# First four tiles loaded with four tokens to a partition, v regrouped by selection matmuls, masks multiplied, new order

## The chip, the cores and the metric

One core of a Trainium2 chip runs the whole program. The metric is the device time of one execution in microseconds. The kernel before takes 180.32 us, the median of three runs (180.25 to 180.33).

## The reference

The program computes attention with a local window and a few global keys, and puts its output through a feed-forward layer that takes the largest of three products.

```python
scores = scale * np.matmul(q, k.transpose(0, 1, 3, 2))
...
is_global = pos[None, :] < int(n_global)
is_local = (rel >= 0) & (rel < int(n_local))
keep = is_global | is_local
dist = np.where(is_global & ~is_local, float(n_local), np.abs(rel).astype(np.float32))
slopes = 2.0 ** (-8.0 * (np.arange(H, dtype=np.float32) + 1) / H)
bias = -slopes[:, None, None] * dist[None, :, :]
...
h = np.maximum(np.maximum(x @ w1, x @ w2), x @ w3)
return (h @ w_out).astype(np.float32)
```

q, k and v are 4 batches x 8 heads x 768 tokens x 64, in float32. n_global is 8 and n_local is 96, so a query sees the 96 keys up to itself and the first eight. The scores get the bias, keys that are not kept get none of the weight, and a softmax follows. The attention output of all heads of a token is a row x of 512. w1, w2, w3 are 512 x 768 and w_out is 768 x 512.

## The kernel before, in words

**Tiles.** The 3072 tokens are 24 tiles of 128, six to a batch. Because the window is shorter than a tile, a tile's queries need two blocks of keys only: the tile itself, and the tile before it, whose first eight keys are overwritten by the batch's first eight (the global ones; `put_kg`, `put_vg`, L209 to L221). Tiles are grouped into chunks for the feed-forward layer: `sizes` 4, 2, 2, 4, 4, 4, 4.

**Order.** There is no scheduler. A string, `SCHEDULE` (L25 on), lists the units one after the other, and a loop at the end (L475) calls the function of each with its numbers. Every engine takes its instructions in that order. The last number of a unit mostly picks the engine that copies: 0 is ACT, 1 is DVE, 2 is POOL (GpSimd). A unit for loads puts its DMA into SP's queue; TensorE's instructions of a later unit wait behind those of an earlier one.

**Units.** The ones that the change and the prediction touch:

- `l` (`load_part`, L151) loads q or k of a group of tiles with `sz` tokens to a partition. Before, the groups begin with two of two tiles, so that a partition's piece in the memory is 512 bytes. `c` (`cast_part`, L178) casts it to bf16; `x` (`u_x`, L226) transposes it on TensorE (L239) and copies it from PSUM with the tokens put back in order (L243) into `qkT`, which holds q and k of a batch with the head's 64 elements across partitions, two heads above each other (`jp` is such a pair of heads).
- `L`, `C`, `X` do the same for single tiles from tile 12 on, with 256-byte pieces; X with a last number of 4 transposes by DMA.
- `v` (`load_v`, L169) loads v of a tile, one token to a partition (256-byte pieces), `C` with a 1 casts it into `va`, which has 65 columns to a head: 64 of v and a one, whose product is the sum of the weights.
- `K` (`u_K`, L297) makes the multiplicative mask of a head, exp of minus slope times distance, with a large distance where a key is not kept. `B` (`u_B`, L291) makes the same as an additive bias.
- `S` (`u_S`, L268) computes a tile's scores for four heads (L283) and takes the exponential (L288). With a last number of 1 it first puts the bias into PSUM by two matmuls with the identity (L275); otherwise `M` (`u_M`, L302) multiplies the mask afterwards. Of the eight half tiles of tiles 0 to 3, six get the bias.
- `A` (`u_A`, L311) multiplies the weights with v (L322, L325), divides by the sums (L331, L332) and leaves `xb`. `T` (`u_XT`, L335) transposes xb into `xT`, on TensorE or by DMA.
- `F` c.f.j (`u_F1`, L355) is a group of four matmuls (L361) of chunk c, for 128 of the 768 columns (f) of weight j. The three results are cast (ACT, L366) and maximised (DVE, L368, L370). `O` (`u_F2`) is the last product (L376) of a tile and its output; `E` the outputs of the last chunk.
- `w` and `W` load and cast the weights: `w`0.j brings the first 256 columns of weight j, `w`1.j the other 512; `o` and `Q` those of w_out.
- `D` issues matmuls on zeros.

**Buffers.** Scores and the products of `A` take turns in two PSUM tiles, `sp0` and `sp1`. All else on TensorE uses three buffers `h` and one `tp`. A matmul into such a buffer waits until its last content was copied out.

Of the kernel before, what the change touches and what calls it, by code (L numbers as in the profile page):

```python
# [12 lines left out]
FP32 = mybir.dt.float32  # L13
# [12 lines left out]
    K0 K1 K2 K3 K4 K5 l1.0 l1.1 D0.3 c0.0.2 B0.1 B1.1 B2.1 B3.0 K6 B4.1 B5.1 c0.1.1 c1.0.2 x0.0.4 B6.1  # L26
    B7.1 x0.1.4 S0.0.1 v0 l2.0 l2.1 K7 S0.1.1 G0.0 S1.0.1 S1.1.0 x1.0.3 c1.1.2 M0.0 M0.1 M1.0 v1 x1.1.4
    C0.1.2 v2 A0.1 G1.2 S2.0.1 M1.1 c2.0.2 x2.0.1 C1.1.1 S2.1.0 G2.2 S3.0.1 M2.0 M2.1 C2.1.1 T0.1 S3.1.1
    M3.0 M3.1 c2.1.2 v3 A1.0 C3.1.0 w0.0 V1.2 x2.1.2 w1.0 A2.1 V2.2 A3.0 T1.0 T2.1 T3.1 W1.0.1 W0.0.0
    G3.2 S4.0.0 S4.1.0 F0.0.0 F0.1.0 M4.0 F0.2.0 F0.3.0 G4.1 S5.0.0 M4.1 S5.1.0 w0.1 W0.1.1 w0.2 W0.2.2  # L30
    V3.2 F0.0.1 F0.1.1 F0.0.2 F0.1.2 v4 C4.1.0 A4.0 V4.2 w1.1 W1.1.2 W2.0.0 F0.4.0 F0.5.0 M5.0 M5.1 w1.2
    W1.2.2 v5 W2.1.0 T4.0 F0.2.1 F0.3.1 l3.0 l3.2 F0.4.1 l3.1 c3.0.2 c3.2.2 F0.5.1 o2 C5.1.0 A5.1 l3.3
    F0.2.2 Q2.2 F0.3.2 W2.2.0 o0 T5.0 F0.4.2 o1 F0.5.2 x3.0.0 F1.0.0 F1.1.0 c3.1.1 F1.2.0 x3.2.0 Q0.2
    F1.0.1 F1.1.1 F1.2.1 l4.0 l4.1 c3.3.0 F1.0.2 F1.1.2 F1.2.2 x3.1.2 x3.3.1 F1.3.0 F1.4.0 Q1.2 F1.3.1
    S6.0.0 S6.1.0 v6 v7 v8 G6.0 F1.3.2 F1.5.0 v9 c4.0.1 F1.4.1 S7.0.0 S7.1.0 G7.2 v10 M6.0 M6.1 M7.0
    M7.1 O0.0.0 F1.4.2 c4.1.1 C6.1.2 C7.1.2 L12 F1.5.1 S8.0.0 S8.1.0 x4.0.0 O0.1.0 A6.0 x4.1.2 A7.1 V7.2
    F1.5.2 v11 T6.0 O0.2.0 T7.1 G8.2 C8.1.2 S9.0.0 S9.1.0 G9.1 v12 v13 O0.3.0 F2.0.0 F2.1.0 S10.0.0 M8.0
    M8.1 M9.0 M9.1 S10.1.0 C9.1.2 L13 L14 F2.0.1 F2.1.1 F2.0.2 A8.0 C12.0.1 F2.1.2 G10.2 O1.0.0 V8.2
    A9.1 X12.1 M10.0 M10.1 C10.1.0 C11.1.0 F2.2.0 S11.0.0 S11.1.0 M11.0 M11.1 L15 F2.3.0 F2.4.0 O1.1.0
    V9.2 A10.1 F2.2.1 V10.2 T8.0 F2.3.1 F2.5.0 T9.0 A11.1 F2.4.1 T10.0 F2.2.2 F2.3.2 T11.1 F2.4.2  # L40
    S12.0.0 S12.1.0 F2.5.1 C13.0.2 C14.0.2 C15.0.1 X13.4 F3.0.0 F3.1.0 F3.0.1 G12.1 C12.1.0 F3.2.0
    F3.1.1 F3.2.1 S13.0.0 S13.1.0 F2.5.2 v14 C13.1.0 C14.1.2 M12.0 M12.1 F3.0.2 F3.1.2 X14.4 F3.2.2
    X15.4 G13.2 M13.0 M13.1 S14.0.0 S14.1.0 F3.3.0 F3.4.0 F3.5.0 M14.0 M14.1 G14.1 A12.0 A13.1 F3.3.1
    F3.4.1 F3.5.1 S15.0.0 M15.0 S15.1.0 G15.0 v15 V13.2 L16 L17 v16 T12.4 v17 M15.1 O2.0.0 C15.1.0 A14.0
    V14.2 F3.3.2 F3.4.2 T13.4 F3.5.2 C16.1.0 C16.0.2 X16.3 T14.4 C17.0.2 A15.1 X17.4 O2.1.0 S16.0.0
    S16.1.0 G16.1 L18 V15.2 L19 T15.1 M16.0 O3.0.0 M16.1 F4.0.0 F4.1.0 F4.0.1 F4.1.1 C18.0.2 L20 C19.0.2
    A16.1 F4.2.0 F4.3.0 S17.0.0 S17.1.0 F4.2.1 F4.0.2 F4.3.1 v18 M17.0 v19 M17.1 X18.3 X19.4 C20.0.0
    V16.2 F4.1.2 C17.1.2 O3.1.1 A17.1 F4.2.2 F4.3.2 S18.0.0 M18.0 S18.1.0 M18.1 F4.4.0 T16.4 T17.4
    F4.4.1 C18.1.2 C19.1.1 F4.4.2 X20.4 G18.1 S19.0.0 S19.1.0 F4.5.0 L21 M19.0 M19.1 v20 F4.5.1 A18.0
    T18.4 F4.5.2 A19.1 T19.4 V19.1 C21.0.1 X21.4 G19.1 L22 C22.0.2 L23 X22.4 O3.2.1 O3.3.0 O4.0.1  # L50
    S20.0.0 S20.1.0 M20.0 G20.0 O4.1.0 F5.0.0 F5.1.0 F5.2.0 S21.0.0 S21.1.0 G21.2 F5.0.1 F5.1.1 M20.1
    M21.0 F5.3.0 F5.0.2 F5.1.2 F5.2.1 F5.2.2 v21 C20.1.1 C21.1.2 F5.4.0 S22.0.0 M21.1 S22.1.0 C23.0.0
    F5.3.1 M22.0 M22.1 F5.5.0 F5.3.2 A20.0 V20.2 G22.2 v22 F5.4.1 X23.4 v23 F5.5.1 T20.4 A21.1 V21.1
    T21.4 F5.4.2 F5.5.2 S23.0.0 S23.1.0 M23.0 O4.2.0 M23.1 C22.1.2 A22.0 C23.1.0 O4.3.0 V22.2 T22.4
    A23.1 T23.4 O5.0.1 O5.1.0 O5.2.1 O5.3.0 F6.0.0 F6.1.0 F6.0.1 F6.0.2 F6.2.0 F6.3.0 F6.4.0 F6.1.1
    F6.2.1 F6.1.2 F6.3.1 F6.4.1 F6.2.2 F6.3.2 F6.5.0 F6.4.2 F6.5.1 F6.5.2 E
# [4 lines left out]
def kernel(  # L61
# [13 lines left out]
    nc = tc.nc  # L75
# [13 lines left out]
    sizes = [4, 2, 2, 4, 4, 4, 4]  # L89

    GROUPS = [[0, 2], [2, 2], [4, 2], [6, 4], [10, 2]]
# [8 lines left out]
    NSTART = sizes[0]  # L100
# [21 lines left out]
    zeros = persist.tile([128, 512], BF16, name="zeros")  # L122
# [3 lines left out]
    bias = persist.tile([128, 2, 2, 2, 3, 128], BF16, name="bias")  # L126
    NVA = 4
    va_ring = [persist.tile([128, H * 65], BF16, name=f"va{i}") for i in range(NVA)]
    va_first = [persist.tile([128, H * 65], BF16, name=f"vaf{i}") for i in range(2)]
    kg8 = [persist.tile([128, NP, NG], BF16, name=f"kg8_{i}") for i in range(2)]  # L130
# [5 lines left out]
    va, masked = {}, {}  # L136
# [7 lines left out]
    def part(n, s):  # L144

        T0, sz = GROUPS[n]
        jn = {2: 4, 4: 2, 6: 1}[sz]
        a, x = divmod(s, 4 // jn)
        return divmod(T0, NT) + (sz, a, x * jn, jn)
# [35 lines left out]
    def cast(T, what, how):  # L185
# [8 lines left out]
        if how == 3:  # L194
            nc.vector.tensor_copy(qk[:, 0], flat[:, 0])
            nc.gpsimd.tensor_copy(qk[:, 1], flat[:, 1])
        else:
            copies[how](qk, flat)  # L198
# [103 lines left out]
    def u_M(T, g):  # L302
        P = Pt[T, g]
        if masked[T, g]:
            return
# [204 lines left out]
```

The softmax here doesn't subtract the row's maximum and nothing guards it: scores larger than these inputs give would overflow.

## Time and profile before

| what | value |
|---|---|
| median of three runs | 180.32 us |
| profiled execution: span from the first to the last instruction | 178.5 us |
| time of the profiled execution itself | not listed apart; its span is 1.8 us short of the median |
| PE busy | 167.1 us, 94% |
| DVE busy | 119.1 us, 67% |
| ACT busy | 103.2 us, 58% |
| POOL busy | 37.4 us, 21% |
| read from HBM | 25.17 MB |
| mean granted TensorE clock | 0.997 |

The profile is of one execution. Its page gives each engine's busy time, the span in 40 slices of 4.46 us with a digit for the busy share in tenths, the DMA queues, the chain of waits (from the last instruction back to what released it, step by step), and groups of instructions with count, busy time, mean duration in ns and the idle time before them. PE are matmuls, PEld weight loads, which run beside them. Matmuls overlap, so that their spacing in the chain tells more than their duration: a 128x512 one lasts 379 ns by the group, while eight in a row take 1.73 us in the chain, 216 ns each.

### The profile page before, as it was taken

The numbers are of one execution on the slowest core, as the hardware profiler recorded it, in microseconds if no ns is written. First come the engines' busy times: TensorE is split into PE (matmuls) and PEld (weight loads), VectorE is DVE, ScalarE is ACT, GpSimd is POOL, SyncE is SP. The second block draws the span as 40 slices with busy tenths as digits, with TensorE's granted clock in tenths as the row PEclk, the third lists the DMA queues.
The fourth block names the chain that finished last, engine by engine and source line by source line (L and its number), as shares of the span: only waits on it lengthen the run. The fifth ranks groups of instructions, "written<-read, shape, count | busy, mean of one in ns | idle before, by whom it ended". The sixth has DMA issues, their size and how long they took to land.

```text
span 178.5 us, 3963 instructions
## 1 busy us (share of the span) xinstructions
PE 167.1 (94%) x1529; PEld 95.9 (54%) x1551; DVE 119.1 (67%) x237; ACT 103.2 (58%) x160; POOL 37.4 (21%) x65
## 2 busy tenths in 40 slices
PE   3599799999999999999999999999999999999991
PEld 0455645458866677845555555454454555444451
DVE  4519975977796689748978448978358986137610
ACT  4867898646689958555753936351862543440131
POOL 4255203543343012210006024100020401000000
PEclk9999999999999999999999999999999999999998
DMA  5999999999998899899544999988989664700015
GB/s 139 292 270 243 357 321 383 319 361 356 252 194 229 218 254 227 142 204 234 92 90 122 167 253 231 145 172 152 182 156 300 123 129 147 252 12 4 0 47 190
DMA packets 83587, 35.52 MB, mean 199 GB/s; under 512 B 66160, under 2 KB 78320, under 8 KB 83568
## 3 DMA queue, kind: packets, MB, share of 16 engines
q1 hardware_dynamic: 83424, 35.20, 83.6%
q8 instruction: 12, 0.20, 0.5%
q10 hardware_dynamic: 144, 0.07, 0.1%
q14 instruction: 7, 0.06, 0.1%
HBM read 25.17 MB, written 6.29 MB: 176 GB/s over the span
## 4 chain that ended last, share of the span: by engine, by line
PE 88%; ACT 3%; DVE 2%; POOL 2%; issue 1%; DMA 1%; POOLq 0%; ACTq 0%
PE h L361 53%; PE po L376 16%; PE sp L283 7%; PE op L322 3%; PE op L325 3%; PE tpp L239 3%; PE xtp L349 2%; ACT wmask L300 2%; PE sp L275 2%; DMA out_dram<-ost 1%; DVE qkT L243 1%; DVE xb L332 1%; ACT ost L382 1%; ACT P L288 1%; PE tp L261 1%
## 5 line engine op out<-in xcount | busy, mean ns | idle before, releaser
L361 PE MATMUL h<-xT,w 128*128 128x512 bf16 (+1 forms) x491 | 99.2, 348 | 0.7 <-issue 0.2
L361 PEld LDWEIGHTS <-w 128*128 128x128 bf16 x504 | 47.0, 98 | 40.4 <-ACT w L427 0.2
L288 ACT ACTIVATE P<-sp 128x1024 bf16<-128x1024 f32 (+1 forms) x48 | 43.4, 954 | 20.4 <-PE sp L283 20.2
L368 DVE TENSOR_TENSOR h<-h,h 128x512 bf16<-128x512 bf16 (+1 forms) x42 | 25.2, 609 | 25.6 <-PE h L361 15.5
L366 ACT CAST h<-h 128x512 bf16<-128x512 f32 (+1 forms) x42 | 21.6, 532 | 21.5 <-PE h L361 21.3
L376 PE MATMUL po<-wo,ht 128*128 128x512 bf16 (+2 forms) x147 | 33.1, 362 | 0.5
L370 DVE TENSOR_TENSOR ht<-h,h 128x512 bf16<-128x512 bf16 (+1 forms) x42 | 25.0, 606 | 3.7 <-PE h L361 3.0
L307 DVE TENSOR_TENSOR P<-P,wmask 128x1024 bf16<-128x1024 bf16 x36 | 24.8, 716 | 3.6 <-ACT P L288 3.5
L382 ACT COPY ost<-po 128x512 f32<-128x512 f32 (+2 forms) x20 | 11.2, 564 | 18.4 <-PE po L376 11.2
L376 PEld LDWEIGHTS <-ht 128*128 128x128 bf16 x156 | 14.0, 98 | 13.8
L332 DVE TENSOR_TENSOR xb<-op,rz 128x512 bf16<-128x512 f32 x24 | 16.6, 691 | 0.8
L283 PEld LDWEIGHTS <-qkT 64*128 64x128 bf16 x352 | 10.2, 96 | 10.0 <-issue 8.0
L283 PE MATMUL sp<-qkT 64*128 64x128 bf16 x352 | 15.2, 223 | 0.4 <-DVE xb L332 0.4
L322 PEld LDWEIGHTS <-P 128*128 128x128 bf16 x192 | 12.5, 97 | 2.7 <-ACT P L288 0.2
L221 POOL COPY va<-vaf 8x260 int32<-8x260 int32 x14 | 6.3, 449 | 34.7 <-PE op L325 34.7
L198 POOL CAST qkb<-raw 128x1024 bf16<-128x1024 f32 x7 | 7.2, 1037 | 27.6 <-DMA raw<-in_k_dram 27.6
L322 PE MATMUL op<-va,P 128*128 128x65 bf16 x160 | 12.4, 193 | 0.3 <-ACT va L189 0.2
L239 PE MATMUL tpp<-identb,qkp 128*128 128x128 bf16 x96 | 8.5, 246 | 4.0 <-POOL qkp L183 3.5
L325 PEld LDWEIGHTS <-P 128*128 128x128 bf16 x160 | 10.4, 97 | 1.8 <-issue 0.2
L239 PEld LDWEIGHTS <-qkp 128*128 128x128 bf16 x96 | 7.0, 112 | 5.8 <-POOL qkp L183 4.4
L325 PE MATMUL op<-va,P 128*128 128x65 bf16 x128 | 9.9, 193 | 0.1
L243 ACT COPY qkT<-tpp 128x1024 bf16<-128x1024 bf16 (+1 forms) x9 | 7.9, 873 | 3.4 <-PE tpp L239 3.4
(66 smaller groups left out, 107.7 us busy)
## 6 DMA issues: line engine op xcount, KB each, us to landing
rawv<-in_v_dram SPq DMA_DIRECT2D x24, 256.0 KB, 4.9
out_dram<-ost SPq DMA_DIRECT2D x23, 256.0 KB, 2.3
rawp<-in_q_dram SPq DMA_DIRECT2D x6, 512.0 KB, 7.3
rawp<-in_k_dram SPq DMA_DIRECT2D x6, 512.0 KB, 7.7
wst<-in_moe_w_dram SPq DMA_DIRECT2D x3, 1024.0 KB, 10.3
raw<-in_q_dram SPq DMA_DIRECT2D x12, 256.0 KB, 4.2
raw<-in_k_dram SPq DMA_DIRECT2D x12, 256.0 KB, 4.7
wst<-in_moe_w_dram SPq DMA_DIRECT2D x3, 512.0 KB, 8.6
```

What stands on the lines that cost most here:

```text
L239: nc.tensor.transpose(tp[:, e, j - lo], qb["p", n, s][:, e, 2 * j:2 * j + 2].rearrange("i h d -> i (h d)"), identb)
L283: nc.tensor.matmul(sp[:, hh, j2, ds], qT(T - ds, 1)[hsl, jp], qT(T, 0)[hsl, jp], start=not how, stop=True, skip_group_check=True)
L288: nc.scalar.activation(P[:, :, 0:n], sp.rearrange("p a b d n -> p (a b) d n")[:, :, 0:n], AF.Exp, bias=0.0, scale=scale)
L307: nc.vector.tensor_mul(P, P, wmask[:, g, :, 0:2])
L322: nc.tensor.matmul(o, P[:, i, 0], heads(va[T])[:, h], start=True, stop=(t == 0), skip_group_check=True)
L325: nc.tensor.matmul(o, P[:, i, 1], heads(va[T - 1])[:, h], start=False, stop=True, skip_group_check=True)
L332: nc.vector.tensor_tensor(out=x.rearrange("p (g h) d -> p g h d", g=2), in0=o4[:, :, :, 0:64], in1=rz[:, :, :, None].to_broadcast([128, 2, ...
L361: nc.tensor.matmul(ps, w123[f // 2][:, dm, j, (f % 2) * 128:(f % 2) * 128 + 128], xT[c][:, dm], start=(dm == 0), stop=(dm == 3))
L366: nc.scalar.copy(h01, ps)
L368: nc.vector.tensor_max(h01s[c, f], h01s[c, f], ps)
L370: nc.vector.tensor_max(ht[c][:, f], h01s[c, f], ps)
L376: nc.tensor.matmul(po, ht[c][:, f, tt * 128:(tt + 1) * 128], wo[:, f, cols], start=(f == 0), stop=(f == NF - 1))
```

## The change

The first group becomes four tiles (0 to 3) with four tokens to a partition: `GROUPS` begins with `[0, 4]`. q and k of it are loaded in eight pieces of a pair of heads, and a partition's piece is 1024 bytes. k is put in order of tokens when it is copied from PSUM, as before; q stays in the order of its four interleaved parts, and the scores' matmuls read 4 x 32 columns of it. v of these tiles is loaded likewise (`y`, `Y`), and a tile's 128 tokens are then picked out by matmuls with a matrix `sel` of zeros and ones, eight of 256 columns to a tile (`z`). New units compute scores and exponentials for two tiles and one pair of heads together (`s`), copy the global keys (`g`) and multiply the masks (`m`, on DVE or POOL). The additive bias is gone: all weights are multiplied with masks, `M` and `m`. `A` may use two `h` buffers instead of a score tile (last number 2).

The first two chunks of four and two tiles become four of two tiles, `sizes` 2, 2, 2, 2, 4, 4, 4, 4; neighbouring ones share their xT and ht tiles. The zeros of `D` shrink, and 36 matmuls of 128 columns stand at the head of TensorE's order, three more a little later. The first two loads move into the order, and all of the order is written anew. Of the later transposes, one tile's q and k, not three, and output transposes of eleven tiles, not thirteen, are left to TensorE; the rest goes by DMA. The function of the last outputs (`E`) stays.

The beginning of the new order, to the first groups of the feed-forward layer:

```
l0.4 l0.5 D5.36 K4 K1 K6 c0.4.1 l0.0 c0.0.2 K5 x0.4.2 c0.5.0 l0.7 K2 g2.0.0 c0.7.2 l0.2 x0.0.3
s0.0.0 K0 l0.6 c0.6.1 c0.2.2 x0.5.1 x0.2.3 K3 g1.0.2 s1.0.0 m1.0.0 x0.6.2 x0.7.3 l0.1 c0.1.2 x0.1.4
g2.1.2 s0.2.1 l0.3 c0.3.2 D1.3 y0 K7 x0.3.3 Y0.2 s0.1.1 m0.1.1 y1 g1.2.1 g2.3.1 s0.3.0 Y1.1 z0.0
m0.2.0 z1.0 g2.2.1 g1.1.1 s1.2.1 m0.0.0 s1.1.0 m0.3.0 A0.2 g1.3.0 A1.2 z2.2 T0.0 w0.0.0 W0.0.2
m1.2.1 s1.3.0 V1.1 m1.3.1 w1.0.0 W2.0.1 w0.1.0 T1.1 z3.0 F0.0.0 F0.5.0 W1.0.1 F0.2.0 m1.1.0 A2.2
V2.0 w0.2.0 W0.1.2 W0.2.0 l1.0 F0.4.0 A3.1 F0.1.0 T2.0 F0.1.1 c1.0.2 l1.1 F0.0.1 c1.1.2 G0.0 F0.0.2
```

The core of the diff:

```diff
-    GROUPS = [[0, 2], [2, 2], [4, 2], [6, 4], [10, 2]]
+    GROUPS = [[0, 4], [4, 2], [6, 4], [10, 2]]
...
+    def u_y(a):
+        r = raw_pool.tile([128, 2 * DM], FP32, name="rawy", tag="raw")
+        raw["y", a] = r.rearrange("i (h x) -> i h x", h=4)
+        nc.sync.dma_start(out=raw["y", a], in_=v[0, 4 * a:4 * a + 4, 0:512, :].rearrange("h (i e) d -> i h (e d)", e=4))
...
+    def u_z(T, how):
+        pool, tag = (psH, "h") if how in (0, 1) else (psT, "tp")
+        ps = pool.tile([128, H, D], FP32, name="vp", tag=tag)
+        for a in range(2):
+            for e in range(4):
+                nc.tensor.matmul(ps[:, 4 * a:4 * a + 4], sel[:, e, 32 * T:32 * T + 32].rearrange("p i e -> p (i e)"),
+                                 qb["y", a][:, :, e], start=(e == 0), stop=(e == 3), skip_group_check=True)
+        va[T] = va_first[0] if T == 0 else va_ring[T % NVA]
+        copies[how % 2](heads(va[T])[:, :, 0:D], ps)
...
-        if how:
-
-            for hh in range(2):
-                nc.tensor.matmul(sp[:, hh, :, 0:n], identb,
-                                 bias[:, g, hh, :, 0:2] if t else bias[:, g, hh, :, 2:3],
-                                 start=True, stop=False, skip_group_check=True)
...
+    def u_s(tp, jp, how):
+
+        sp = psS.tile([128, 2, 4, 128], FP32, name="sp", tag=f"sp{how}")
+        g, j2 = divmod(jp, 2)
+        tiles = (2 * tp, 2 * tp + 1)
+        lo = 0 if tp else 1
+        for i, T in enumerate(tiles):
+            for ds in range(2 if T else 1):
+                for hh in range(2):
+                    hsl = slice(64 * hh, 64 * hh + 64)
+                    qs = qkT[0][hsl, 0, jp, 0:512].rearrange("c (e i) -> c e i", e=4)[:, :, 32 * T:32 * T + 32]
+                    ks = k2x[hsl, jp] if T - ds == 2 and ds else qT(T - ds, 1)[hsl, jp]
+                    nc.tensor.matmul(sp[:, hh, 2 * i + ds if T else 1], ks, qs,
+                                     start=True, stop=True, skip_group_check=True)
+        if tp:
+            if "P1" not in Pt:
+                Pt["P1"] = stage_pool.tile([128, 4, 2, 4, 128], BF16, name="P1", tag="wst1")
+            P = Pt["P1"][:, jp]
+        else:
+            P = p_pool.tile([128, 2, 4, 128], BF16, name="P0", tag="P")
+        Pt["s", tp, jp] = P
+        for hh in range(1 + lo):
+            o, x = (P[:, hh, 1:4], sp[:, hh, 1:4]) if lo else (P.rearrange("p h b n -> p (h b) n"),
+                                                               sp.rearrange("p h b n -> p (h b) n"))
+            nc.scalar.activation(o.rearrange("p b (i e) -> p b i e", e=4), x.rearrange("p b (e i) -> p b i e", e=4),
+                                 AF.Exp, bias=0.0, scale=scale)
+
+    def u_m(tp, jp, how):
+        g, j2 = divmod(jp, 2)
+        P = Pt["s", tp, jp]
+        mul = (nc.vector, nc.gpsimd)[how].tensor_mul
+        if tp:
+            wm = wmask[:, g, j2::2, 1:3].rearrange("p a s n -> p a (s n)")[:, :, None].to_broadcast([128, 2, 2, 256])
+            Pv = P.rearrange("p h (i s) n -> p h i (s n)", i=2)
+            mul(Pv, Pv, wm)
+        else:
+            mul(P[:, :, 1:4], P[:, :, 1:4], wmask[:, g, j2::2])
...
-            nc.tensor.matmul(wp, zeros[:, 0:128], zeros, start=True, stop=True)
+            nc.tensor.matmul(wp[:, 0:128], zeros, zeros, start=True, stop=True)
...
-        load_part(0, 0)
-        load_part(0, {2: 1, 4: 2, 6: 4}[GROUPS[0][1]])
...
+        nc.vector.memset(sel, 0.0)
+        for e in range(4):
+            nc.vector.tensor_copy(sel[:, e, :, e], identb)
```

## The prediction

> **What bounds the kernel now.** I read first the page's busy shares and slices, then the busy time by stretches, then the waits, then single queues. The page:
>
> ```profile
> PE 167.1 (94%) x1529; PEld 95.9 (54%) x1551; DVE 119.1 (67%) x237; ACT 103.2 (58%) x160; POOL 37.4 (21%) x65
> PE   3599799999999999999999999999999999999991
> DMA  5999999999998899899544999988989664700015
> ```
>
> TensorE is the bound from the fifth slice on; only the first few are thin. I cut the span where TensorE stops waiting for attention of the first four tiles (22.68 us: scores of tile 4, then the first FFN group) and where its last matmul but the tail's ends (172.04 us):
>
> ```profile
> 0.00:22.68 22.68, 16.15 (x191) 9.96 (x191) 14.22 (x40) 16.60 (x27) 9.27 (x23) 1.00 1.07 262
> 22.68:172.04 149.36, 148.15 (x1317) 84.11 (x1337) 104.60 (x196) 84.29 (x129) 28.14 (x42) 1.00 0.83 191
> 172.04:178.48 6.44, 2.75 (x24) 1.83 (x23) 0.29 (x1) 2.30 (x5) 0.00 (x0) 0.91 0.46 163
> ```
>
> The columns are PE, PEld, DVE, ACT, POOL. The middle 149.36 us is full, and the waits of PE between 23 and 170 us are this one line:
>
> ```profile
> PE h L361 <- issue: 0.2, 1, 0.2
> ```
>
> So the change can gain in three places only: the first 22.68 us, TensorE's amount of work after it, and the tail. What TensorE really did by 22.68 us, at the spacings of the chain of waits when warm (128-wide transposes 0.45 per 8, scores 0.55 per 16, 65-wide products 0.26 per 8), is small: 48 transposes 2.7, 56 scores 1.9, 12 bias matmuls 2.2, 56 products 1.7, 16 output transposes 0.9, in all 9.4 us. Some 13.3 us are lost there.
>
> **What the Trainium skill says.** "TensorE: Matmul & The Clock Gate", What's actually happening: an idle TensorE runs at half clock and needs about 3.4 us of activity to reach full. The trace agrees: eight transposes take 1.01 us at 7.69 and 0.45 at 41.04. "DMA: Bandwidth & Descriptors", Why small descriptors are slow: a fixed cost per packet. The trace agrees; four stretches in which 512, 256, 1024 and 2048 byte packets prevail moved (last column, GB/s):
>
> ```profile
> 5.00:9.00 4.00, 2.34 (x18) 1.80 (x18) 2.21 (x6) 3.22 (x8) 1.34 (x2) 1.00 1.21 290
> 15.00:17.00 2.00, 1.63 (x26) 0.93 (x26) 1.97 (x5) 1.61 (x2) 0.61 (x2) 1.00 1.35 222
> 23.00:25.00 2.00, 1.95 (x20) 0.95 (x16) 1.23 (x3) 1.93 (x3) 0.00 (x0) 1.00 1.10 347
> 28.00:31.00 3.00, 3.00 (x20) 1.44 (x19) 2.06 (x3) 2.79 (x4) 0.48 (x2) 1.00 1.05 387
> ```
>
> "SBUF — State Buffer", SBUF: two separate sides: GpSimd and a VectorE instruction with two SBUF inputs (or a fast copy) exclude each other for a whole instruction. The trace agrees, in the queues of POOL and DVE:
>
> ```profile
> 31.93 1.03 POOL L427 CAST w<-wst 128x1024 bf16<-128x1024 f32 x1
> 32.48 1.63 DVE L307 TENSOR_TENSOR P<-P,wmask 128x1024 bf16<-128x1024 bf16 x2
> ...
> 41.24 1.04 POOL L430 CAST wo<-wost 128x1024 bf16<-128x1024 f32 x1 [1.80 <-DMA wost<-in_moe_w_out_dram]
> 41.68 1.15 DVE L183 CAST qkp<-rawp 128x1024 bf16<-128x1024 f32 x1
> ```
>
> The DVE cast takes 0.69 elsewhere, here 1.15: it ends 0.55 after POOL's. The fourth place is a price: "GPSIMD Engine Reference", Elementwise, about 2.6 cycles per element at 1.2 GHz for two inputs.
>
> **Durations used**, from the groups with shapes kept apart:
>
> ```profile
> L288 ACT ACTIVATE P<-sp 128x1024 bf16<-128x1024 f32 x40 | 39.0, 1027 | 15.3 <-PE sp L283 15.1
> L307 DVE TENSOR_TENSOR P<-P,wmask 128x1024 bf16<-128x1024 bf16 x36 | 24.8, 716 | 3.6 <-ACT P L288 3.5
> L189 ACT CAST va<-rawv 128x512 bf16<-128x512 f32 x9 | 5.4, 630 | 0.4 <-DMA rawv<-in_v_dram 0.2
> L300 ACT ACTIVATE wmask<-rbase 128x384 bf16<-128x384 f32 x8 | 3.6, 509 | 1.5 <-DVE rbase L470 1.5
> ```
>
> Six of the last kind take 2.59 us together in ACT's queue, so a full ACT spends each duration less 0.09.
>
> **The change, part by part.** *Loads.* q and k of four tiles: 2.1 MB at 347 instead of 290 GB/s, 6.0 for 7.2 us; v of four tiles 1.05 MB at 347 instead of 222, 3.0 for 4.7. q, k of tiles 4 and 5 also move behind the first four weight loads. Packets start at 2 us, landing is seen some 0.9 us after the last byte: q, k all in at 9.6, v at 12.7, then weights at 14.2, 17.0, 18.5, 20.0. Before, v of tile 3 was cast at 19.77, just in. The loads alone would let the second weight block's matmuls start near 19.6: they leave 5 us. I count nothing for them until the engines are asked, since those come later. Behind them SP's queue gets two more X and two more T transposes by DMA, late, where loads lead their casts by several us: nothing.
>
> *Start of the constants.* The select matrix adds to DVE, ahead of `rbase`, a memset of 1024 words (256 take 0.27, so 1.07, less 0.2 for the smaller `zeros`) and four copies (about 0.1 each as queued). `rbase` was ready for ACT at 3.76; now about 4.65. 36 warm-up matmuls (0.107 cold, 3.9 us) run while TensorE has nothing else: nothing, and the clock is full at about 5 us.
>
> *ACT up to the exponentials of tiles 2, 3.* In its order: 8 masks at 0.42, 3 copies at 0.49, a cast 0.53, small key copies 0.65, eight 384-wide exponentials at 0.42, four 1024-wide at 0.93, three v copies at 0.5, one xT copy 0.5: 3.4+1.5+0.5+0.6+3.4+3.7+1.5+0.5 = 15.1. From 4.65 it ends at 19.75 if it never waits. Strided PSUM reads add nothing: L243's, also strided, take 1.02 per 1024. The bias work of ACT and DVE goes (2.5 us), the mask multiplies come.
>
> *Masks.* Eight: five on DVE (0.56 for 768 elements, 0.69 to 0.72 for 1024), three on POOL, which no row shows. Bounds for 1024: 1.04 (POOL's cast of one input) and 2.25 with the skill's price; I take 2.25, and 1.7 for 768. The last one (jp 3) starts after the last exponential and stands before tile 2's product in TensorE's order. Behind that product wait F0.4, tile 3's product, F0.1, T2.
>
> *The port.* At 13.9 POOL's first multiply starts and holds back two of DVE's (m0.0, m0.3) until 15.6: they end at 16.7, not at 15.3, where the first product could go; through xb and T0 this puts ACT's last exponential at 20.3 instead of 19.75. At 20.3 DVE has a weight cast (0.69) and a multiply (0.72) to do against POOL's 2.25; one after the other 3.66. Tile 2's product starts at 24.0; without the exclusion at 19.8+2.25 = 22.05.
>
> *TensorE's work.* From tile 2's product to F0.1.1: 0.47+0.44+0.47+0.44+0.22 = 2.04. What then remains is before's 149.36, plus what before had done (16 transposes 0.90, T3 0.22), less five FFN groups already done (20 matmuls at 0.109, 2.18), less 16+8 transposes given to DMA (1.35), plus 0.1 for narrower FFN chunks: 147.06. The bias matmuls removed (2.2) and the 32 selection matmuls added (256 wide, 0.109, 3.5) both lie ahead, where TensorE waits. Tail 6.44, as before: O's evacuations are unchanged. Outside the span: 180.32 is the median; the profiled execution's span is 178.48, 1.84 less, kept.
>
> Sum: time = start of tile 2's product + 2.04 + 147.06 + 6.44 + 1.84 = that start + 157.38. Par is a start at 22.94. With 24.0: **181.4 us**.
>
> *Placed at nothing:* the two-tile exponentials of tiles 2, 3 lie in one of the three wide weight staging buffers, so the third wide weight load waits at SP for tile 3's product (near 25.5), and v of tile 5 and all later loads wait behind it; by the byte count the queue is busy with earlier loads until about 28, which hides it. Chunks of two tiles raise ACT by six times 0.19 (two 256-wide casts of 0.39 for one of 0.59) and DVE by six times 0.30 (four of 0.42 for two of 0.69), beside 24 us where ACT had 16.3 and DVE 17.9 busy (25 to 49 us); if their queues delay PSUM buffers, some tenths. The last transpose by DMA is covered by 18 output matmuls (3.9, before 5.2) against 0.20+0.69+2.4 = 3.3; without cover at most 0.5.
>
> **Rivals.** *Not slower: no collision.* DVE's and POOL's instructions miss each other; the start is 22.05 and the time 179.4, with POOL's low bound 1.04 it is 178.2. For it: only two clear collisions in 60 us before. Against: POOL then multiplied nothing. It decides at a sum of last exponential and multiply of 22.94. *Faster: ACT alone.* If the multiply costs no more than DVE's 0.7, the start is 20.5: 177.9. For it: loads leave room. Against: the price. *Slower still: cold clock.* Between 5 and 18 us TensorE has little to do; should it be at half clock when F0 begins, 3.4 us pass at half rate, 1.7 more: 183.1. For it: it was cold until about 13 before. Against: the warm-up and the selection matmuls. *The larger packets do nothing* is no case of its own: it is the first sum, in which engines and not loads set the start.
>
> **Numbers.** Collision 0.38 (180.7 to 182.5); none 0.28 (178.2 to 180.6: 0.17 faster, 0.08 the same, 0.03 slower); ACT alone 0.20 (177.2 to 178.4); cold clock 0.14 (182.5 to 184). Faster by over 0.2% (what a measurement can tell, 0.36 us) 0.37, within 0.08, slower 0.55. Range 177.9 to 183.2: it leaves out half of the third case and half of the last, 0.17. The likeliest case's own range is 180.7 to 182.5.
>
> **What would show it.** Right: the last exponential of the two-tile scores ends near 20, POOL multiplies of over 2 us, DVE multiplies stretched beside them, and tile 2's product at 24, PE waiting for it; from there no PE waits. Wrong: PE full from before 22.9 us, POOL multiplies near 1 us, waits of PE after 30 us, or ACT idle before 20.

## The result

The changed kernel takes 186.38 us (median of 4 runs, 185.64 to 186.80), the kernel before 180.32 (180.25 to 180.49): 1.033 times as long, interval 1.030 to 1.035. The forecast was 181.4, its range ended at 183.2. Run a second time beside other kernels the change took 186.22 (185.69 to 186.79), 1.032 (1.031 to 1.034) of the kernel before; "186.3" below means these two. Executions that lay over 1.5% above the fastest of the same kernel are left out of the ratios to the kernel before (two of six of e2_half_pool, the traced one among them, three of six of e4_before_mul, one of six of e6_order and of f2_bias, four of six of h1_split, whose ratio so rests on two), while medians are of all executions.

The profiled execution took 185.64 with a span of 183.9. The page's lines on TensorE, the granted clock and the DMA engines:

```profile
PE 173.1 (94%) x1655; PEld 107.8 (59%) x1655; DVE 129.1 (70%) x272; ACT 100.1 (54%) x170; POOL 48.4 (26%) x73
PE   7589979999999999999999999989999999999992
PEclk9957999999999999999999999999999999999999
```

TensorE's share is again 94%. VectorE is busy 10 us longer than before, GpSimd 11; by the table at the end of this section, about 6.8 of VectorE's 10 are time in which it is held up inside an instruction. The granted clock was down between 9 and 18 us. The stretches, cut where the prediction cut them: at F0.1.1 and at the last output matmul before the tail (columns as there):

```profile
0.00:26.87 26.87, 21.59 (x247) 16.90 (x248) 17.94 (x55) 19.76 (x41) 16.45 (x28) 0.87 0.99 304
26.87:177.50 150.63, 148.65 (x1386) 89.02 (x1384) 110.89 (x217) 78.04 (x125) 31.99 (x46) 1.00 0.85 180
177.50:183.90 6.40, 2.83 (x25) 1.83 (x23) 0.29 (x1) 2.30 (x5) 0.00 (x0) 0.95 0.46 164
```

The prediction had 26.04, 147.06 and 6.44 here. So the start is 0.83 late, the tail is right, and 3.57 us are lost in the middle, where I had expected none. Before, the waits of PE in that stretch were a single line of 0.2; now they are:

```profile
PE h L449 <- DVE ht L462: 1.0, 2, 0.5
PE op L398 <- DVE P L381: 0.4, 1, 0.4
PE h L449 <- DVE xT L437: 0.2, 1, 0.2
PE h L449 <- DVE w L524: 0.2, 1, 0.2
```

All four are behind VectorE. This view counts only a part of the lost time. Measured from the starts of TensorE's matmuls, less the usual distance to the next one, the stalls of over 0.1 are 0.40 at 29.7 us, 0.35 at 37.0, 0.60 at 55.2, 0.62 at 68.9, 0.16 at 73.0, 0.19 at 94.9, 0.69 at 123.2 and 0.29 at 159.4. They sum to 3.30 of the 3.57.

**The start** in the queues of GpSimd, VectorE and TensorE:

```profile
13.56 3.12 PE L227 MATMUL vp<-yb,sel 128*128 128x256 bf16 x16
14.21 1.76 POOL L365 TENSOR_TENSOR P<-P,wmask 128x768 bf16<-128x768 bf16 x1 [1.32 <-ACT P L353]
14.39 1.62 DVE L326 COPY k2x<-qkT 128x120 bf16<-128x120 bf16 x1
15.91 1.03 POOL L524 CAST w<-wst 128x1024 bf16<-128x1024 f32 x1
15.94 1.03 DVE L327 COPY k2x<-qkT 128x8 bf16<-128x8 bf16 x1
...
22.00 2.79 POOL L363 TENSOR_TENSOR P<-P,wmask 128x1024 bf16<-128x1024 bf16 x1 [1.48 <-ACT P L353]
24.84 0.20 PE L398 MATMUL op<-va,P 128*128 128x65 bf16 x1 [1.26 <-POOL P L363]
```

Two copies of 120 and 8 elements, elsewhere 0.18 and 0.16, take 2.65 us: each ends with the GpSimd instruction beside it. The selection matmuls run at a granted clock of 0.60 and take 0.195 each. The last line is the wait that the prediction named: the last four of tile 2's sixteen products stand behind GpSimd's last multiply until 24.84. The other twelve had run from 23.06 on.

**A stall of the middle**, 0.62 at 68.9 us, seen in the two queues:

```profile
66.31 1.04 POOL L527 CAST wo<-wost 128x1024 bf16<-128x1024 f32 x1
66.39 2.11 DVE L381 TENSOR_TENSOR P<-P,wmask 128x1024 bf16<-128x1024 bf16 x2
68.42 1.07 DVE L462 TENSOR_TENSOR ht<-h01s,h 128x256 bf16<-128x256 bf16 x3
```

Two mask multiplies that nobody needs yet start beside a cast of GpSimd and take 0.8 longer than the 1.29 that they need when undisturbed (e8_half_late below). Behind them in VectorE's queue stands the max of the last line, and TensorE's next matmul waits until it has freed a PSUM buffer.

How long VectorE was held can be summed: for each of its instructions, I take the time beyond the lower quartile of its own operation and shape in the same trace, where that is over 0.15 us. "Again" is the second trace of the changed kernel, f5_again.

| kernel | held before 26.5 us | held after | time, us (ratio times 180.4) |
|---|---|---|---|
| before | 0.8 | 1.4 | 180.4 |
| changed | 3.4 (again: 3.1) | 5.6 (again: 6.4) | 186.3 |
| g1_half_casts | 3.2 | 2.5 | 184.3 |
| g3_half_all | 2.1 | 3.1 | 182.8 |
| e4_before_mul | 1.5 | 3.8 | 183.4 |

### The profile page after: what moved, and what is told of

Read it like the earlier page. It is cut to its first block, busy times and chain, and to the rows that moved or that the text cites. A ratio compares the mean times of both kernels' runs of the same rounds, so it can differ in the third digit from the quotient of the medians.

```text
span 183.9 us, 4240 instructions
## 1 busy us (share of the span) xinstructions
PE 173.1 (94%) x1655; PEld 107.8 (59%) x1655; DVE 129.1 (70%) x272; ACT 100.1 (54%) x170; POOL 48.4 (26%) x73
## 3 DMA queue, kind: packets, MB, share of 16 engines
HBM read 25.17 MB, written 6.29 MB: 171 GB/s over the span
## 4 chain that ended last, share of the span: by engine, by line
PE 74%; DVE 13%; ACT 6%; POOL 2%; issue 2%; DMA 1%; DVEq 0%; ACTq 0%; POOLq 0%
PE h L449 44%; PE po L469 15%; PE sp L313 5%; PE op L398 3%; DVE P L381 3%; DVE ht L462 2%; PE op L401 2%; PE tpp L271 2%; ACT wmask L376 2%; POOL P L363 2%; ACT P L353 1%; ACT P L317 1%; DMA out_dram<-ost 1%; PE xtp L436 1%; DVE h01s L460 1%
## 5 line engine op out<-in xcount | busy, mean ns | idle before, releaser
L449 PE MATMUL h<-xT,w 128*128 128x256 bf16 (+1 forms) x576 | 101.6, 326 | 1.7 <-DVE ht L462 1.0
L449 PEld LDWEIGHTS <-w 128*128 128x128 bf16 x576 | 53.8, 98 | 38.2 <-issue 3.1
L317 ACT ACTIVATE P<-sp 128x1024 bf16<-128x1024 f32 (+1 forms) x40 | 36.4, 961 | 17.3 <-PE sp L313 17.3
L460 DVE TENSOR_TENSOR h<-h,h 128x512 bf16<-128x512 bf16 x24 | 16.3, 684 | 15.6 <-PE h L449 15.6
L458 ACT CAST h<-h 128x512 bf16<-128x512 f32 x24 | 14.0, 587 | 22.1 <-PE h L449 22.0
L462 DVE TENSOR_TENSOR ht<-h,h 128x512 bf16<-128x512 bf16 x24 | 16.3, 684 | 2.9 <-PE h L449 2.0
L460 DVE TENSOR_TENSOR h01s<-h01s,h 128x256 bf16<-128x256 bf16 x24 | 9.8, 417 | 5.1 <-PE h L449 2.8
L475 DVE COPY ost<-po 128x512 f32<-128x512 f32 (+1 forms) x10 | 6.5, 650 | 9.8 <-PE po L469 9.8
L195 POOL CAST qkp<-rawp 128x1024 bf16<-128x1024 f32 (+1 forms) x11 | 9.6, 886 | 5.8 <-DMA rawp<-in_q_dram 3.3
L462 DVE TENSOR_TENSOR ht<-h01s,h 128x256 bf16<-128x256 bf16 x24 | 9.6, 415 | 1.2 <-PE h L449 0.8
```

Source lines behind the costliest of these rows:

```text
L317: nc.scalar.activation(P[:, :, 0:n], sp.rearrange("p a b d n -> p (a b) d n")[:, :, 0:n], AF.Exp, bias=0.0, scale=scale)
L449: nc.tensor.matmul(ps, w123[f // 2][:, dm, j, (f % 2) * 128:(f % 2) * 128 + 128], xT[B][:, dm, o], start=(dm == 0), stop=(dm == 3))
L458: nc.scalar.copy(h01, ps)
L460: nc.vector.tensor_max(h01, h01, ps)
L462: nc.vector.tensor_max(ht[B][:, f, o], h01, ps)
L475: copy(ost, po)
```

## The experiments

The theory is that GpSimd's instructions, the three multiplies at the start and its casts later, keep VectorE waiting, and that TensorE then stands behind VectorE's queue. I call this waiting of the two engines for each other the lock. The rivals are VectorE's amount of work with two-tile groups, masks multiplied at all, the loads, and the clock.

**GpSimd at the start: e2_half_pool.** GpSimd multiplies one of the two heads of a pair; VectorE's multiplies stay whole:

```
+        if how:
...
+                Pv = P.rearrange("p h (i s) n -> p h i (s n)", i=2)[:, 0:1]
...
+                mul(P[:, 0:1, 1:4], P[:, 0:1, 1:4], wmask[:, g, j2::2][:, 0:1])
```

> The changed kernel with GpSimd's three mask multiplies cut to half of their elements (384, 512, 512); it leaves half of the masks of these head pairs out. Everything stays in its place in every queue. Theory A, as predicted: the start is set by GpSimd's last multiply and by what its lock does to VectorE; each multiply halves to about 1.0, tile 2's products no longer wait 1.4 at 23.4 us, the key copies of VectorE at 14.4 and 15.9 shorten, and the time falls by 1.4 to 2.2 us, to about 184.5. Rival, ScalarE's queue or TensorE's clock sets the start: under 0.5 us.

The ratio to the kernel before is 1.016 (1.013 to 1.018), which is 183.2: 3.0 us below the change, more than expected. The multiplies took 1.31, 1.16 and 1.52 us, and TensorE waited 0.33 instead of 1.42 for the last of them; g3_half_all below, with the same edit, has 1.26, 1.16, 1.52 and 0.33. So GpSimd sets the start. The edit cuts GpSimd's own work and its hold on VectorE together, so it doesn't tell which of the two counts more. Nor is it shown where all of the 3.0 come from: F0.1.1 came 0.87 earlier than in the changed kernel in this trace (an execution of 185.91 us, with a stall of 1.32 at 36.9), and 2.1 earlier in g3's trace than in g1's.

**The lock later: e8_half_late, g1_half_casts, against g2_half_max.** In e8 GpSimd's casts of `wo` (and, it was meant, of some q, k) are halved. In g1 its casts of the weights but the first, of q, k of tiles 4 to 11 and of `wo` are halved. In g2 it is VectorE's own work that is cut. The kernels leave the other halves out:

```
+        copies[how](wo[:, 2 * i:2 * i + 1], wst["o", i][:, 0:1])                    # e8, g1
+            qk, src = qk[:, 0:sz // 2], src[:, 0:sz // 2]                           # g1
+        copies[how](w123[g][:, 0:m, j], src[:, 0:m])                                # g1, m = 2 of 4
+            nc.vector.tensor_max(h01[:, 0:n], h01[:, 0:n], ps[:, 0:n])              # g2, n = 128 of 256; ht likewise
```

> The changed kernel with GpSimd's casts of q, k of tiles 6 to 9 and of the output weights cut to half (0.55 us for 1.04); it leaves the other halves out, and transposes and output matmuls read the first half twice. No queue changes its order or its owner. Theory A, the exclusion of the two engines makes the stalls at 55.2 and 68.9 us: the multiplies beside these casts shorten by 0.4 to 0.5 each, the stalls shrink to under 0.2, and the time falls by 0.6 to 1.2 us, to about 185.4. Theory B, VectorE's amount of work in this order: the stalls stay, and the time changes by less than 0.4 us.

1.027 (1.025 to 1.028), median 185.17. The q, k part of the edit did nothing: those parts (tiles 10, 11, not 6 to 9) hold two tiles, and the slice took both. So the run holds its own control: one stall whose cast was halved, and two whose casts were not. Beside the halved `wo` cast:

```profile
66.23 0.62 POOL L530 CAST wo<-wost 128x512 bf16<-128x512 f32 x1
66.73 1.29 DVE L384 TENSOR_TENSOR P<-P,wmask 128x1024 bf16<-128x1024 bf16 x2
```

The multiplies are no longer held and the stall of 0.62 is gone; the untouched ones at 55 and 123 us stay at 0.60 and 0.71.

> The changed kernel with every GpSimd cast of weights (but the first), of q, k parts of tiles 4 to 11 and of the output weights cut to half (0.55 for 1.04 us); it leaves the other halves out, and TensorE reads the first halves twice. Order, VectorE's and ScalarE's work are untouched. Lock theory: the multiplies and casts of VectorE beside them shorten, the stalls near 37, 55 and 69 us (0.35 to 1.22, 0.59, 0.62) shrink to 0.2 or less each, the one near 123 stays (its cast is not halved), and the time falls by 1.5 to 2.4 us from 186.3. Amount theory (VectorE has too much to do with two-tile groups): the stalls shift and the time falls by less than 0.6.

1.022 (1.019 to 1.024), 184.32: 2.0 us less. The stalls at 37 and 69 us are gone, the one at 55 is 0.16. All waits of PE between 27 and 178 us:

```profile
PE h L452 <- DMA xT<-xb: 0.2, 1, 0.2
```

The stall at 123, whose cast wasn't cut, went too, and the queues show why: the two multiplies, at 119.22, now came before the cast, and it was GpSimd that took longer (1.36 for 1.04).

> The changed kernel with VectorE's 48 max instructions of the first two chunks on 128 of 256 columns; it leaves the others out. That takes some 0.13 us from each, in all about 3 us of VectorE between 27 and 70 us, which is more than the two-tile groups added (six times 0.30). GpSimd's casts stay. Amount theory: the stalls near 37, 55 and 69 us go, and the time falls by 1.5 to 2.4 us. Lock theory: a stretched multiply stands ahead of TensorE's next need all the same, and the time falls by less than 0.8.

1.031 (1.029 to 1.034), 185.71: 0.6 less, which the intervals don't tell from no change. The stall near 37 us is down to 0.14, but those at 55, 69 and 123 us stay (0.60, 0.51, 0.57), as the lock theory has it:

```profile
PE h L449 <- DVE ht L463: 0.8, 2, 0.4
PE op L398 <- DVE P L381: 0.4, 1, 0.4
```

**Both: g3_half_all**, e2 and g1 in one.

> e2_half_pool and g1_half_casts together: GpSimd's three multiplies and its casts halved. If the start's loss and the later one are separate and both GpSimd's, the gains add: 3.0 and 1.5 to 2.4, so 181 to 182, within 1 us of the kernel before. If one only uncovers the other, no better than 183.3, where e2_half_pool was.

1.013 (1.010 to 1.016), 182.90: 3.4 us of the 5.9 are back, not the 5.0 that the two gave alone. By the prediction's own sum its profiled execution (tile 2's last products delayed 0.33 to 23.11, so a start of 22.78) should take 22.78 + 157.38 = 180.2, and it took 181.76; stalls of 0.32, 0.16, 0.16, 0.18 and 0.33 remain after the start and explain 1.2 of the 1.6. VectorE is still held for 5.2 us. The median lies 1.1 above this execution, and no trace shows where the others lose it.

**By order instead: e6_order, e1_late_act.** e6 moves what TensorE needs ahead of the multiplies:

```
-M9.1 M10.1 F3.2.0 F3.5.2      +F3.2.0 F3.5.2 M9.1 M10.1
-M17.0 M17.1 F5.2.2            +F5.2.2 M17.0 M17.1
-S5.0 M4.1 S5.1 W1.1.1         +W1.1.1 S5.0 M4.1 S5.1
-F2.3.2 A7.1 F2.1.1 F2.0.2     +F2.3.2 F2.1.1 F2.0.2 A7.1      (and G3.1 -> G3.0)
```

> The changed kernel with six units moved and nothing else: what TensorE needs next (a weight cast, a max of the first layer, the products of tile 7) goes ahead of the mask multiplies that nobody waits for yet, and one small key copy goes from VectorE to ScalarE. If the later loss is TensorE standing behind stretched multiplies in VectorE's queue, the stalls at 29.7, 37.0, 55.2, 68.9 and 123.2 us (0.40, 0.35, 0.60, 0.62, 0.69) go, and the time falls by 1.5 to 2.5 us, to about 184.3. If VectorE's sum of work is the limit, the stalls come back a little later and the time falls by less than 0.6 us.

1.030 (1.027 to 1.034), median 186.20: nothing that can be measured. The stalls at 30 and 123 went, the one at 69 fell to 0.24; but 0.47 at 36.9, 0.26 at 54.3 and 0.75 at 56.8 (tile 7's transposes, now right behind its products) came in their place. VectorE was held for 4.4 us later on: a moved unit meets another cast.

> The changed kernel with five later GpSimd casts (two of q, k of tiles 6 to 9, two of the output weights, one of tile 21) given to ScalarE; order and VectorE's work untouched. Theory A, GpSimd's casts hold VectorE's mask multiplies back at 53.5, 66.4 and 121.0 us, and TensorE stalls behind them for 0.60, 0.62 and 0.69: the multiplies take 0.7 each, these three stalls go, and the time falls by 1.5 to 1.9 us, to about 184.7. Theory B, VectorE simply has too much to do in this order (two-tile groups, one more multiply per score group): multiplies shorten, but TensorE still waits at these places, and the time stays at 186 or above, more if ScalarE is delayed by the five casts (5 us).

1.052 (1.047 to 1.057), 189.77: slower by 3.5. The stalls named in the expectation are gone, but others took their place, since TensorE now waits for the five casts in ScalarE's queue:

```profile
PE po L469 <- ACT wo L527: 1.7, 1, 1.7
PE tpp L271 <- ACT qkp L195: 1.7, 2, 1.2
```

**Masks multiplied: e4_before_mul, e5_bias, f2_bias, e7_both, f3_bias_order, f4_m_dve.** e4 takes the bias matmuls out of the kernel before (`S0.0.1` becomes `S0.0.0`, and so on; no `B`).

> The kernel before with one part of the change: scores of tiles 0 to 3 take no bias matmuls, all their masks are multiplied on VectorE in the units that stand there for it. 12 matmuls and the eight bias tiles go, six multiplies come (two of 0.42, four of 0.69, in sum 3.6 us), of which about 2.1 us fall into 13 to 22.7 us, where VectorE was full. Theory A, VectorE limits that stretch: slower by 0.8 to 1.8 us, about 181.6. Rival, TensorE's 2.2 us of bias matmuls are on the path: faster by up to 1 us.

1.017 (1.015 to 1.019), that is 183.4: 3.0 us slower, more than I expected. Two multiplies of 512 elements, 0.42 each, took 1.53 beside GpSimd, and the products of tile 0 waited for them. After that VectorE had work without a break, as its 10.90 busy us (the third engine) in the 11 from 13 to 24 us show, and the first layer began at 25.94 for 23.27. TensorE's waits there, 1.6, 1.1 and 0.3, are all behind VectorE. Only about 0.7 us of VectorE's time is the lock; here it is above all its amount of work, as theory A of the expectation has it:

```profile
13.53 1.53 DVE L309 TENSOR_TENSOR P<-P,wmask 128x512 bf16<-128x512 bf16 x2
...
14.78 0.74 PE L322 MATMUL op<-vaf,P 128*128 128x65 bf16 x8 [1.58 <-DVE P L309]
...
13.00:24.00 11.00, 7.92 (x113) 6.16 (x112) 10.90 (x20) 5.79 (x7) 3.17 (x6) 1.00 1.17 307
```

In the changed kernel the same part can be undone. e5 and f2 add the masks by TensorE:

```
+            nc.tensor.matmul(o, identb, bt, start=True, stop=False, skip_group_check=True)
-                                     start=True, stop=True, skip_group_check=True)
+                                     start=False, stop=True, skip_group_check=True)
 (no m units; K units after F0.1.1; B units at the start)
```

> The changed kernel with one part undone: the masks of the first four tiles are added by TensorE again (16 matmuls with the identity, 384 or 512 wide, from bias tiles that VectorE makes between 4.6 and 7.2 us, where it is idle), the eight multiplies are gone, and the eight mask tiles of ScalarE are made after the start, since only tile 4 needs them. Theory A, the multiplies on GpSimd and VectorE, and ScalarE's queue, set the start: tile 2's products, which waited until 24.84, go by about 21.5, and the time falls by 2.5 to 4 us, to about 183. Rival, the start is set by loads or by a TensorE at half clock, on which the 16 matmuls cost up to 6 us: no gain, or slower than the changed kernel.

1.094 (1.092 to 1.096), 197.38: slower for a reason of its own. The bias tiles were written straight into the scores' order, each next element 32 further, and that took VectorE 13.47 us for eight, where f2's neighbouring elements took 1.31 for three:

```profile
4.93 13.47 DVE L385 TENSOR_SCALAR wo<-rbase 128x384 bf16<-128x384 f32 x8
```

> Both edits together: bias matmuls for the first four tiles and the six moved units. If the start and the later stalls are two separate losses, the gains add: 4 to 6 us off the changed kernel, 180.5 to 182, near the kernel before. If the earlier start only moves the later stalls, the sum is no better than the larger of the two.

This is e5 with e6's moves: 1.095 (1.093 to 1.096). It has the same loss and says nothing more.

> The masks of the first four tiles added by TensorE again, as in e5_bias, but the eight bias tiles are made from a copy of the distances that ScalarE has put in the order of the scores once, so that each reads and writes neighbouring elements (0.29 us each on VectorE in the kernel before, 0.5 on ScalarE, where e5_bias took 1.68 each). Theory A, the multiplies set the start: tile 2's products go by about 21.5 for 24.84, the time falls by 2.5 to 4 us from the changed kernel, to about 183. Rival, loads or a TensorE at half clock set it: within 1 us of the changed kernel.

1.034 (1.031 to 1.036), median 186.50: no gain. The wait for GpSimd is gone (tile 2's products run through from 24.1), but the first layer begins at 22.78, 1.0 later: from 13.6 us on TensorE itself has scores, bias matmuls (0.6 for two) and selection matmuls one after the other, and is never idle for long. F0.1.1 is 0.41 earlier than in the changed kernel. TensorE ran at full rate here, so that the first two tiles' selection matmuls took 1.92 for 3.12 us, and it didn't help:

```profile
14.94 1.92 PE L229 MATMUL vp<-yb,sel 128*128 128x256 bf16 x16
```

> f2_bias with five of the six moved units of e6_order (tile 7's products one group later only) and one copy of v rows given from VectorE to GpSimd. If the later stalls can be taken out by order once the start is early: 1 to 2 us below f2_bias, 181 to 182. If VectorE's sum of work between 25 and 70 us is the limit, an earlier start only leaves it less time: no better than f2_bias.

1.036 (1.034 to 1.037), 187.13: no better than f2.

> The changed kernel with GpSimd's three mask multiplies done by VectorE (0.55, 0.7 and 0.7 us for 1.76, 2.12 and 2.79), the last of them behind the copy of tile 1's transposes, and one copy of v rows given to GpSimd. Masks are still multiplied. If GpSimd's price and its lock are the loss: tile 2's products go by about 23.3 for 24.84, the time falls by 1 to 2 us, to about 185. If multiplying at all is the loss, since VectorE is then full instead: less than 0.8 us.

The edit turns `m0.1.1` into `m0.1.0` and so on. 1.052 (1.049 to 1.055), 189.65: slower by 3.3, and not for the multiplies' price. The first of them stands in VectorE's queue ahead of v's cast and waits for ScalarE's exponential (1.09); the selection matmuls then wait 1.9 for that cast, and the clock is near half from 9 to 20 us. An order by which VectorE never waits for ScalarE wasn't tried, so this doesn't separate price from place.

**Loads: e3_v_old, g4_bias_v_old.** `y0 Y0.2 z0.0` and their like become `v0 v1`, `C0.1.0`.

> The changed kernel with v of the first four tiles loaded and cast as before (four loads in 256 byte pieces, four casts on ScalarE in the place of the four copies), without the 32 selection matmuls and the two casts of 1024. If the selection path does what the larger packets promise, this is slower: loads end 1.7 us later, so the time rises by up to 1.7 us. As I predicted the loads (they lead the engines) it costs nothing: within 0.5 us of the changed kernel. If the selection matmuls (cold, 3.1 us from 13.6) and the casts hold the products of tiles 0 and 1 back, it is faster by 0.5 to 1 us.

1.042 (1.039 to 1.046), 187.96: 1.7 slower. The first layer waits for tile 1's xT copy on VectorE, which stands behind a weight cast, and that cast waits for its load. But the trace doesn't make the load the cause, for the two instructions come at nearly the same times in the changed kernel (first two lines) and here (last two):

```profile
20.60 0.68 DVE L524 CAST w<-wst 128x1024 bf16<-128x1024 f32 x1
21.20 0.40 DVE L437 COPY xT<-xtp 128x512 bf16<-128x512 bf16 x1
...
20.35 1.02 DVE L524 CAST w<-wst 128x1024 bf16<-128x1024 f32 x1 [1.51 <-DMA wst<-in_moe_w_dram]
21.29 0.41 DVE L437 COPY xT<-xtp 128x512 bf16<-128x512 bf16 x1
```

The first layer begins at 21.85, for 21.75. What differs is TensorE: without the selection matmuls it waited 3.0 us for that copy, the granted clock was 0.50 from 17 to 23 us, eight matmuls of the first layer took 1.87 where twelve take 1.47 in the changed kernel, and F0.1.1 came 0.78 later. A stall of 1.32 at 38.5 follows; the two traces of the changed kernel have 0.35 and 1.22 there. How the 1.7 of the median divides between the clock and such stalls stays open.

> f2_bias with v of the first four tiles loaded and cast as before: two parts of the change undone (masks by TensorE, v without selection matmuls), the order, the four-token groups of q, k and the two-tile chunks kept. If TensorE itself is the limit of f2_bias' start (its 32 selection matmuls, 4.0 us, and 16 bias matmuls lie one after the other from 13.6 to 23 us), the first layer begins 1.5 to 3 us earlier and the time falls to about 184. If loads limit it then, or TensorE is at half clock without those matmuls, as it was in e3_v_old, no gain: 186 to 188.

1.032 (1.031 to 1.034), 186.19: with masks on TensorE too, the old loads cost nothing. The first layer starts at 21.49, after a wait of 1.39 for VectorE's xT copy, and F0.1.1 comes at 25.17:

```profile
21.49 1.47 PE L464 MATMUL h<-xT,w 128*128 128x256 bf16 x12 [1.22 <-DVE xT L452]
...
25.17 1.03 PE L464 MATMUL h<-xT,w 128*128 128x256 bf16 x8
```

So the start is 1.7 us earlier than in the changed kernel, and the time is still the same: the stalls after it sum to 4.8 us instead of 3.3, the first of them 0.94 at 28.5, again for an xT copy of VectorE. What the start gained was lost again in stalls.

**The change again: f5_again.**

> The changed kernel itself once more, as the measure for the three others on the same chip. 185.6 to 186.8 as before; its profile shows how far the stalls move from one execution to the next: the starts of GpSimd's casts follow the landing of loads, so I expect the stalls near 37 us to differ by several tenths and the one near 23.4 us to be there again with 1.2 to 1.5.

186.22. Its profiled execution has a span of 185.0, 1.1 more than the first. The start is 0.28 later (24.84 became 25.12), and the stall near 37 us is 1.22 instead of 0.35. There TensorE waits for a weight cast of VectorE that stands behind two mask multiplies. Two casts of GpSimd, which start when a load lands, began at 34.28 for 33.20, fell beside both multiplies, and stretched them to 2.87 us from 1.99. So the executions of the changed kernel differ by 1.1 us, where those of the kernel before stayed within 0.3 beside them.

**Shorter instructions: h1_split, h2_before_split.** GpSimd does its whole work in pieces of some 256 elements, on the changed kernel and on the one before:

```
+        for x in range(m):
+            s = slice(x * d // m, (x + 1) * d // m)
...
+                nc.gpsimd.tensor_copy(out[:, s], in_[:, s])
```

> The changed kernel with every GpSimd cast of 1024 or 512 elements and every GpSimd multiply done in instructions of some 256 (multiplies of 768: 384) elements; the whole work is done. If VectorE waits for the end of the one GpSimd instruction that runs, it now waits 0.3 us instead of up to 1.0 or 1.6: the stalls near 37, 55, 69 and 123 us shrink to 0.3 or less, the key copies at 14.4 and 15.9 us shorten, GpSimd's sum rises by 0.1 per added instruction, and the time falls by 1 to 2.5 us from 186.3, to about 184.5. If VectorE doesn't get in between two queued GpSimd instructions, nothing is gained, and GpSimd's longer sum makes it 0.3 to 1 us slower.

1.039 (1.036 to 1.043); the six executions take 186.76 to 192.80, median 191.06, and none is clearly below the changed kernel. The trace, of the 186.76, is worth reading all the same. These are all waits of PE from 26 to 178 us:

```profile
PE h L478 <- DVE xT L466: 2.7, 1, 2.7
PE h L478 <- DMA xT<-xb: 0.4, 1, 0.4
PE h L478 <- issue: 0.2, 1, 0.2
```

The stalls near 37, 55, 69 and 123 us are gone, as expected if VectorE comes in between the pieces. At the start it does so too: the copy of 8 elements that took 1.03 beside a whole cast takes 0.40 beside four quarters in a row. But once it doesn't, and that costs 2.8 us:

```profile
15.71 2.09 POOL L201 CAST w<-wst 128x256 bf16<-128x256 f32 x4
15.73 0.40 DVE L345 COPY k2x<-qkT 128x8 bf16<-128x8 bf16 x1
...
26.33 2.82 POOL L199 CAST qkp<-rawp 128x256 bf16<-128x256 f32 x8
28.44 2.81 DVE L266 COPY qkT<-kg 128x32 bf16<-128x32 bf16 x1
29.09 0.76 POOL L201 CAST va<-rawv 128x256 bf16<-128x256 f32 x2
29.77 1.45 POOL L201 CAST w<-wst 128x256 bf16<-128x256 f32 x4
31.15 0.39 POOL L190 COPY va<-vaf 8x260 int32<-8x260 int32 x1
```

The copy of 32 elements outlasts eight quarter casts and ends at 31.25, when GpSimd has just gone over to another operation. After TensorE's idle time the granted clock was 0.50 from 31.6 to 34.2 us, which costs another 1.1. After 26.5 us VectorE is held for 4.7 us in all; 2.6 of it is this one copy, and the 2.0 that are left stand against 5.6 and 6.4 in the changed kernel. So in this trace splitting frees VectorE nearly everywhere, and one long hold takes the gain back. When VectorE comes in and when not isn't shown, and the executions of up to 192.80 have no trace.

> The kernel before with its GpSimd casts of 1024 and 512 elements done in instructions of 256. Its later multiplies collide too (at 32.5, 41.7 us), but TensorE waits nowhere after 22.7 us, so nothing can be gained there; before 22.7 us the copies at 13.3 and 16.4 us (1.82 for two, 1.22 for one of 0.68) may shorten. I expect 179.9 to 180.4, at most 0.3% below the kernel before.

1.0021 (1.0012 to 1.0030), 180.84: 0.4 us slower, with a stall of 0.45 at 34.4 that the kernel before doesn't have. No kernel here beats the one before.

## Why the prediction was wrong

- **Sign and start: right, 0.8 short, in part by luck.** The kernel is slower, by the wait named: tile 2's products behind GpSimd's multiply. By terms: the first products went at 17.56, not 16.7, because two small copies took 2.65, which I had not looked for, and the selection matmuls, which I had put where TensorE waits anyway, took 3.12 for the 1.75 that 16 times 0.109 gives; ScalarE waited 0.59, 0.65 and 0.60 us for them at 15.5, 16.7 and 19.9. So the last exponential ended at 21.92, not 20.3. GpSimd's multiply then took 2.79, its own 2.12 and 0.67 of one VectorE multiply, not 3.66, since VectorE's cast had already run. One error is 1.6 late, the other 0.8 short, and they partly cancel. The 2.04 behind the start came out as 2.03, but twelve of the sixteen products in it had run before, and short waits stood in their place.
- **GpSimd's price: right.** The trace has 1.76 (1.66 in f5) for 768 elements and 2.12 for 1024, against 1.7 and 2.25 that the prediction worked out from the Trainium skill, "GPSIMD Engine Reference", Elementwise.
- **"From there no PE waits", and what follows the start "placed at nothing": wrong.** This is the step that failed: 3.3 us of stalls, where "some tenths" were allowed. The prediction itself had named waits of PE after 30 us as a sign of being wrong. I weighed VectorE's and ScalarE's work in the later stretch as sums beside the time there was, although the two collisions that I showed from the kernel before had already told that VectorE's instructions don't keep their length beside GpSimd. The changed order puts casts of GpSimd beside multiplies at more places, holds VectorE 4 to 5 us longer, and has TensorE's next need directly behind. g1 gives 2.0 us of it to the lock. For the max instructions of the two-tile groups g2 leaves 0.6, which is within the noise.
- **Later transposes by DMA: "without cover at most 0.5".** It cost 0.29 at 159.4 us and 0.40 the second time. The size was right, but it was placed at nothing; in e3 and g4 the stall there is 0.81 and 0.88.
- **Work, tail and outside: right.** The middle, 150.63 less 3.30 of stalls, is 147.3 for 147.06; the tail is 6.40 for 6.44, and the time outside the span 1.74 for 1.84.
- **Loads at nothing: right as far as shown.** With the old loads of v the first layer begins only 0.1 later (e3). The 1.7 us that e3 loses come after that, with TensorE at half clock, and with masks on TensorE (g4) nothing is lost. No run undoes the larger pieces of q and k.
- **The rival of a cold clock: not so, as it was put.** TensorE ran at full rate at the first layer. It was slower earlier, and runs in which it wasn't don't begin sooner: in f5 the first two tiles' selection matmuls took 2.69, and TensorE then waited 0.41 for a held key copy; in f2 they took 1.92, but bias matmuls stand beside them there. So what the slow start cost by itself isn't shown.
- **The sum.** 181.4 + 0.83 at the start + 3.57 in the middle - 0.04 in the tail - 0.10 outside = 185.66, the profiled 185.64. The median is 0.7 higher. The other trace of the changed kernel took 186.79, and its start 0.28 later and its stall near 37 us 0.87 larger make up that difference.

Open: the 2.5 us between g3 and the kernel before, of which the trace lists about 1.2 as stalls; how much of the loss at the start is GpSimd's own time and how much its lock; what the two-tile chunks cost beyond their max instructions; and which order would avoid the casts.

## What to carry to other kernels

Before moving work from an idle TensorE to VectorE or GpSimd, list for every GpSimd instruction which instructions of VectorE fall beside it that copy or that read two inputs from SBUF, and what TensorE needs directly behind them; shares of busy time don't show it. When one part of a change is undone and the time stays, look at where the gain went: in g4 the start came 1.7 us earlier and the stalls behind it grew by 1.5. A median alone would have called the part harmless, as it would have called h1's splitting useless. A new order needs its waits costed, not only its sums.

## What the runs showed of the hardware

- A VectorE copy of 8 elements took 1.03 us beside a GpSimd cast (0.16 elsewhere), one of 32 took 2.81 beside a row of quarter casts; VectorE's max with one operand in PSUM kept its 0.42 there (27.57, two in 0.79).
- The exclusion works in both directions: a GpSimd multiply of 1024 took 2.12, and 2.79 where VectorE had a multiply beside it; a GpSimd cast took 1.36 for 1.04 (g1).
- In the Trainium skill, "SBUF — State Buffer", SBUF: two separate sides, has the exclusion for a whole instruction. Most collisions shown here agree: a held copy ends with the one GpSimd instruction beside it, even where the next follows at once (at 16.0 in the changed kernel), and shorter instructions hold for less (0.40 for 1.03 in h1). Twice it outlasted several: eight quarter casts at 28.44 in h1, and two whole casts in e4, where a multiply that began at 35.16 took 2.01.
- The granted clock alone doesn't show TensorE's rate: in g1 it reads 1.00 from 11 to 17 us, and the 16 selection matmuls take 3.21 us all the same, where f2's take 1.92. The spacing of the matmuls does.
- A permuting VectorE instruction over 384 elements (reading neighbours in float32, writing each next one 32 further) took 1.68 us, one that also writes neighbours 0.44 (0.29 in the kernel before). ScalarE made a copy in the same permuted order in 0.85.
